# VectorE clips the decays ahead of five of its eight memsets and copies both halves of four heads' queries; heads are turned at the pace of the scores

## The chip, the cores and the metric

The kernel runs on one core of one Trainium2 chip. The metric is the time of one execution in microseconds (us) on the device. Five engines work in parallel, each through its own queue in order: PE (TensorE, matrix products), ACT (ScalarE), DVE (VectorE), POOL (GpSimd) and SP (SyncE, which here only issues transfers). PEld is the loading of weights into PE.

## The reference

Decay attention over 8 batches of 8 heads, 576 positions and 64 dimensions, followed by a two-layer block with a maximum of three products:

```python
def _attn_ref(q, k, v, f):
    scale = 1.0 / np.sqrt(D)
    scores = scale * np.matmul(q, k.transpose(0, 1, 3, 2))
    log_f = np.log(np.clip(f, 0.0001, 1.0))
    cum = np.cumsum(log_f, axis=-1)
    decay = cum[:, :, :, None] - cum[:, :, None, :]
    scores = np.where(causal, -1000000000.0, scores + decay)
    scores = scores - np.max(scores, axis=-1, keepdims=True)
    attn = np.exp(scores)
    attn = attn / (np.sum(attn, axis=-1, keepdims=True) + 1e-09)
    return np.matmul(attn, v)

def _moe_ref(x, w1, w2, w3, w_out):      # x: 4608 x 512, w1..w3: 512 x 768, w_out: 768 x 512
    h = np.maximum(np.maximum(x @ w1, x @ w2), x @ w3)
    return h @ w_out
```

## The kernel before

The program is written as a list of steps. Each step names its engine, an assumed cost, what it reads and writes, and a priority (smaller goes first). A planner (`Plan.emit`) replays the list against these costs, takes on each engine the ready step of the lowest rank, and writes all steps out in order of their planned starts. The queues then run in exactly that order. So one moved priority or dependency changes the order on every engine around it.

The first eight heads (batch 0) go a way of their own. `load_raw` brings a head's keys and queries as they lie in memory (raw tiles, w_111 for head 0 to w_118 for head 7). `turn_head` turns them on PE (L473) into four banks of the accumulator: for even heads queries in mp_130 and keys in mp_131, for odd heads queries in mp_132 and keys in t. Four copies take the two halves of each (e = 0, 1) to the head's tile: before, DVE takes the first half of the queries (L481), ACT the other three (L483). The heads' tiles are qs_65 (head 0), qs_66, ks_67, ks_68 (heads 1 to 3), xh (4, 5) and xl (6, 7). The lower half of each key tile is cleared by a DVE memset (L409), and one of its rows takes the summed decays: for heads 0 and 1 by ACT (L433), for the others by a small transfer (L440) from u_91, which DVE writes at L436.

The decays (pf_80) come from `decay`: two loads, a clip on DVE (L424), a logarithm on ACT (L426), a running sum ("scan") on DVE (L429). ACT loads its tables for logarithm and exponential ahead of need (L421, L428).

Scores of a head are made in two units: unit 2 has queries 0 to 255, unit 1 the rest, in batch 0 in two parts, b (banks s_126, s_127) and then a (bank s_125). Each is: products and mask on PE (L647, L663), maximum over banks on DVE (L702 to L707), maximum over partitions on POOL (L717), a correcting product on PE (L647, from gm_84, gm_85, ph_71 or pl_72), exponentials on ACT (L735), and values on PE (L772), copied out by ACT (L784, and the row of sums L786).

Meanwhile the weights of the two-layer block arrive (L511, tiles w_95 to w_118 in order) and are split into a rounded part and a remainder: ACT L515, DVE L517 and L519, ACT L522, DVE L523. The block's products (L964, L993) are mixed with the attention from then on. The keys and queries of the second batch come as hl, are transposed by DVE (L536) and split (ACT L540, DVE L542). V is loaded by L368, for each pair of heads once the first head's key tile is complete.

Twenty warm-up products (L453, on the identity, into bank s_125) carry priority 90: the planner puts one wherever it believes that PE would be idle. All twenty stand ahead of the first scores in that bank, those of head 0's part a.

Of the kernel before, what the change touches and what calls it, by code (L numbers as in the profile page):

```python
# [48 lines left out]
class Plan:  # L49
# [18 lines left out]
    def add(self, eng, cost, fn, r=(), w=(), prio=0.0, xfer=0.0, rows=128, short=0.0, light=False):  # L68
        i = len(self.steps)
        r, w = ([p for k in keys for p in self.parts.get(k, [k])] for keys in (r, w))  # L70
        deps = set()
        for k in r:
            if k in self.wrote:
                deps.add(self.wrote[k])
        for k in w:
            if k in self.wrote:
                deps.add(self.wrote[k])
            deps.update(self.read.pop(k, ()))
        for k in w:
            self.wrote[k] = i  # L80
        for k in r:
            if k not in w:
                self.read.setdefault(k, set()).add(i)
        deps.discard(i)
        self.steps.append((eng, cost, fn, deps, prio, xfer, rows, short, light))
# [86 lines left out]
def act_cost(cols):  # L172
    return 0.833 * cols + 60


def dve_cost(cols):
    return 1.04 * cols + 68
# [3 lines left out]
def kernel(  # L181
# [15 lines left out]
    nc = tc.nc  # L197
    B, H, S, D = q.shape
    DM, DFF = w1.shape
    P = 128  # L200
# [40 lines left out]
    add = plan.add  # L241
# [9 lines left out]
    KF, QF = [x[:, 0:S] for x in KQ], [x[:, S:] for x in KQ]  # L251
# [115 lines left out]
    def dma(dst, src, r=(), w=(), prio=0.0, bytes_=300000):  # L367
        add("SP", 475 if bytes_ > 200000 else 640, lambda: nc.sync.dma_start(out=dst, in_=src), r, w, prio, bytes_ / 360)  # L368
# [10 lines left out]
    def first_constants(i):  # L379
        nc.gpsimd.memset(QF[i][64:P, :], 1.0)  # L380

    def head_constants(i, prio):

        for key, ns, go in (
# [4 lines left out]
        ):  # L389
            add("POOL", ns, go, w=[key], prio=prio)  # L390

    def value_constants():
        for vn in VN:
            nc.gpsimd.memset(vn[64:P, :, 4, :], 0.0)
            nc.gpsimd.memset(vn[:, :, :, D:D + 1], 1.0)
# [10 lines left out]
    add("POOL", 100, lambda: nc.gpsimd.memset(LESS[0:1].bitcast(F32), -1.0), w=["less"], prio=-9)  # L406
    for i in range(H):
        add("POOL", 525, lambda i=i: first_constants(i), w=[f"qf{i}/2"], prio=-9 + i)
        add("DVE", 605, lambda i=i: nc.vector.memset(KF[i][64:P, :], 0.0), w=[f"kf{i}/2"], prio=-5.5 + 0.1 * i)  # L409
    add("POOL", 1650, value_constants, w=[f"vn{i}" for i in range(4)], prio=-8)  # L410


    def decay():

        fx, lx = PF[1][0:BH + 1, 0:S], PF[1][0:BH + 1, S:2 * S]
        ft = fx[0:BH]
        cs = CS
        fs = f.rearrange("b h s -> (b h) s")

        add("DVE", 60, lambda: nc.vector.memset(TM[0][0:1, 0:1], 1.0), [], ["tm0"], DP)  # L420
        add("ACT", 1400, lambda: nc.scalar.activation(TM[0][0:1, 0:1], TM[0][0:1, 0:1], AF.Ln), ["tm0"], ["tm0"], DP)  # L421
        dma(ft, fs, w=["pf1/0"], prio=DP)
        dma(fx[BH:BH + 1], fs[1:2], w=["pf1/1"], prio=DP, bytes_=2304)
        add("DVE", 440, lambda: nc.vector.tensor_scalar(fx, fx, 1e-4, 1.0, op0=ALU.max, op1=ALU.min),  # L424
            ["pf1"], ["pf1"], DP)
        add("ACT", 600, lambda: nc.scalar.activation(lx, fx, AF.Ln), ["pf1"], ["pf1", "ln"], DP)  # L426

        add("ACT", 1400, lambda: nc.scalar.activation(TM[0][0:1, 0:1], TM[0][0:1, 0:1], AF.Exp), ["ln", "tm0"], ["tm0"], DP)  # L428
        add("DVE", 1275, lambda: nc.vector.tensor_tensor_scan(  # L429
            fx, lx, lx, 0.0, op0=ALU.add, op1=ALU.bypass),  # L430
            ["pf1"], ["pf1"], DP)
        for n in range(2):
            add("ACT", act_cost(S), lambda n=n: nc.scalar.activation(  # L433
                KF[n][D:D + 1, :], fx[BH * n:BH * n + 1, :], AF.Copy, scale=-1.0 / scale), ["pf1"], [f"kf{n}/2"], DP)
        c8 = UT[KT - 1][0:H, :]
        add("DVE", 540, lambda: nc.vector.tensor_scalar(c8, ft[0:H, :], -1.0 / scale, None, op0=ALU.mult),  # L436
            ["pf1"], [f"u{KT - 1}"], DP)
        for n, e, dst in [(n, n + 1, KF[n][64:65, :]) for n in (2, 3)] + [
                (4 + 2 * i, 6 + 2 * i, x[64:65, :, 0:S]) for i, x in enumerate(PAIRS)]:
            add("SP", 560, lambda n=n, e=e, dst=dst: nc.sync.dma_start(out=dst, in_=c8[n:e, :]),  # L440
                [f"u{KT - 1}"], [f"kf{x}/2" for x in range(n, e)], ROWS + n, 2304 / 360)
        add("DVE", 369, lambda: nc.vector.tensor_scalar(cs[:, 0, :], ft, -1.0, None, op0=ALU.mult),
            ["pf1"], ["cs"], DP)
        add("DVE", 669, lambda: nc.vector.scalar_tensor_tensor(
            cs[:, 1, :], ft, -1.0, cs[:, 0, :].bitcast(F32), op0=ALU.mult, op1=ALU.subtract),
            ["pf1", "cs"], ["cs"], DP)
        dma(cdram.bitcast(F32), cs.bitcast(F32), ["cs"], ["cdram"], DP + 3)

    def warm_up():

        z = ident.rearrange("p (o x) -> p o x", o=1).broadcast_to((P, 4, P))
        for _ in range(20):
            add("PE", 217, lambda: nc.tensor.matmul(SP1[0].rearrange("p (o x) -> p o x", o=4), ident, z, start=True, stop=True),  # L453
                ["const"], ["sp1/0"], 90)
        add("DVE", 165, lambda: nc.vector.tensor_copy(IDF, ident), ["const"], ["idf"], -6)
# [8 lines left out]
    def turn_head(n, prio):  # L464


        for c, buf, kc in ((0, QF, "qf"), (1, KF, "kf")):
            ps, kp = ((MPS[0], "mp0"), (MPS[1], "mp1"), (MPS[2], "mp2"), (TPS, "t0"))[2 * (n % 2) + c]

            def go(ps=ps, c=c):  # L470
                for x in range(3):
                    for e in range(2):
                        nc.tensor.matmul(  # L473
                            ps[D * e:D * e + D, 0:288].rearrange("d (p x) -> d x p", x=3)[:, x],
                            RAWQK[n][:, c, e, D * x:D * x + D], IDF[0:96, 0:96], start=x == 0, stop=True, skip_group_check=True)

            add("PE", 700, go, [f"raw{n}/{c}", "idf"], [kp], prio, rows=96)
            for e in range(2):
                dst, src = buf[n][0:D, 288 * e:288 * e + 288], ps[D * e:D * e + D, 0:288]
                if c == 0 and e == 0:  # L480
                    add("DVE", dve_cost(288), lambda dst=dst, src=src: nc.vector.tensor_copy(dst, src), [kp], [f"{kc}{n}/0"], prio)  # L481
                else:
                    add("ACT", act_cost(288) + 115 * e, lambda dst=dst, src=src: nc.scalar.activation(  # L483
                        dst, src, AF.Copy), [kp], [f"{kc}{n}/{e}"], prio)
# [64 lines left out]
    def load_v(pi, prio):  # L549
        b, pr = pi // NP, pi % NP  # L550
        src = v[b, 2 * pr:2 * pr + 2]
        i = pi if b < NB32 else vbuf(pi)
        vn, kv = VN[i], f"vn{i}"

        after = [f"kf{2 * pi}"] if b < NB32 else ["qs0/0"]
        for j in range(2):
            dma(vn[:, j, 0:4, 0:D], src[j, 0:512, :].rearrange("(c p) d -> p c d", p=P),
                after, [kv + f"/{j}"], prio, 262144)
        dma(vn[0:64, :, 4, 0:D], src[:, 512:S, :].rearrange("h p d -> p h d"), after, [kv + "/2"], prio)
# [471 lines left out]
    LEAD, MLAG, WP, WR = 2.1, -0.1, 0.7, 0.65  # L1031
    DP = -10.9
    DPW = 9.0
    ROWS = -4.0
    warm_up()
    decay()
    QP = -0.3
    UO = 1
# [7 lines left out]
    for n in range(H):  # L1046
        load_raw(n, n - 8.9)
    for n in range(H):
        turn_head(n, n - 5.6)
        if n % 2 == 0:  # L1050
            load_v(n // 2, n - LEAD - VP)
    for unit, up in ((2, 0.0), (1, 0.1)):
# [94 lines left out]
```

## Time and profile before

| what | value |
|---|---|
| median of 3 runs | 903.28 us |
| lowest, highest | 903.13, 905.31 us |
| span of the profiled execution | 900.3 us |
| PE busy | 889.3 us (99%) |
| DVE, ACT, POOL busy | 624.8, 389.0, 425.8 us |
| transfers | 110.99 MB, mean 123 GB/s |

The profile is of one execution on one core; its span runs from the first to the last instruction. For the profiled execution no other time than its span is given; the median of the runs is 3.0 us above it. Rows of a timeline show the start in us, the duration in us, the engine, the line, the operation, what is written and read, how many instructions of a kind were merged, and in brackets how long the engine had been idle before and what ended that. Rows of waits show the total in us, how often, and the longest.

### The profile page before, as it was taken

To read this page: it belongs to the slowest core of one execution; us is meant where nothing else is said; L and a number is where in the kernel's file an instruction comes from. 1 tells how busy PE (TensorE), PEld (TensorE's weight loads), DVE (VectorE), ACT (ScalarE), POOL (GpSimd) and SP (SyncE) were. 2 spreads that over 40 slices of the span, in tenths; PEclk is the share of its full clock that TensorE was granted. 3 is DMA by queue.
4 is the path that set the end of the run, shared out by engine and by line. 5 is a ranking of instruction groups with operands and counts; after the bars stand their busy time and mean duration, and the time that the engine had idled before them with its cause. 6 is when DMAs were issued, how large, how long until landed. Compare 5 with 4: busy or idle time off the path is not lost.

```text
span 900.3 us, 18339 instructions
## 1 busy us (share of the span) xinstructions
PE 889.3 (99%) x6646; PEld 804.0 (89%) x6646; DVE 624.8 (69%) x1419; ACT 389.0 (43%) x904; POOL 425.8 (47%) x380
## 2 busy tenths in 40 slices
PE   8999999999999999999999999999999999999998
PEld 6899989888889899989989998998989898998998
DVE  6999954667759786877849787786958677672211
ACT  6898543433334443443334443344433533442111
POOL 4543232245555756556464755555565564650000
PEclk9999999999999999999999999999999999999999
DMA  7994265554464454446445445536434555401000
GB/s 197 316 270 133 56 159 131 147 135 127 99 189 96 124 136 118 126 100 169 96 124 149 117 133 138 140 93 181 95 102 123 126 149 118 105 15 37 1 36 24
DMA packets 98155, 110.99 MB, mean 123 GB/s; under 512 B 52637, under 2 KB 65693, under 8 KB 98066
## 3 DMA queue, kind: packets, MB, share of 16 engines
q1 hardware_dynamic: 98066, 109.83, 46.7%
q8 instruction: 53, 0.87, 0.4%
q14 instruction: 36, 0.29, 0.1%
HBM read 50.22 MB, written 9.87 MB: 67 GB/s over the span
## 4 chain that ended last, share of the span: by engine, by line
PE 92%; ACT 3%; DMA 1%; DVE 1%; SPq 1%; issue 1%; DVEq 0%; ACTq 0%
PE mp L964 51%; PE mp L993 17%; PE s L647 12%; PE t L803 9%; PE t L772 2%; PE t L822 1%; DMA w<-in_moe_w_dram 1%; ACT w L515 1%; ACT pf L735 1%; SPq L368 1%; DMA r_r<-rdram 0%; ACT ph L786 0%; ACT w_r L522 0%; PE s L663 0%; ACT u L784 0%
## 5 line engine op out<-in xcount | busy, mean ns | idle before, releaser
L964 PE MATMUL mp<-xh_r,w_r 128*128 128x320 f32 (+1 forms) x2160 | 463.5, 298 | 1.7 <-DVE tm L973 1.4
L964 PEld LDWEIGHTS mp<-xh_r,w_r 128*128 128x128 f32 x2160 | 356.1, 188 | 11.2 <-issue 5.6
L964 PE MATMUL mp<-xl_r,w_r 128*128 128x320 f32 (+1 forms) x1080 | 319.6, 296 | 0.4 <-DVE xl_r L940 0.4
L759 POOL PARTITION_ALL_REDUCE z<-va_s x96 | 194.9, 2030 | 158.4 <-DVE va_s L751 57.4
L717 POOL PARTITION_ALL_REDUCE gm<-mx x131 | 156.6, 1196 | 206.8 <-DVE mx L707 88.9
L964 PEld LDWEIGHTS mp<-xl_r,w_r 128*128 128x128 f32 x1080 | 203.3, 188 | 1.1 <-DVE xl_r L940 0.6
L973 DVE TENSOR_TENSOR tm<-mp,tm 128x256 f32<-128x256 f32 (+1 forms) x192 | 86.5, 451 | 84.6 <-PE mp L964 79.4
L647 PE MATMUL s<-qs_r,ks_r 128*128 128x320 f32 (+4 forms) x784 | 133.1, 284 | 0.2 <-issue 0.2
L647 PEld LDWEIGHTS s<-qs_r,ks_r 128*128 128x128 f32 (+1 forms) x784 | 116.9, 181 | 18.2 <-issue 13.4
L993 PE MATMUL mp<-w_r,hmh_r 128*128 128x512 f32 (+1 forms) x396 | 122.7, 392 | 0.0
L707 DVE TENSOR_TENSOR mx<-mx,s 128x320 f32<-128x320 f32 (+3 forms) x248 | 92.3, 372 | 19.5 <-PE s L647 6.9
L993 PEld LDWEIGHTS mp<-w_r,hmh_r 128*128 128x128 f32 x396 | 70.2, 188 | 13.2 <-issue 1.4
L976 ACT ACTIVATE hmh_r<-tm 128x256 fp32r<-128x256 f32 x96 | 39.9, 416 | 97.0 <-DVE tm L973 96.1
L993 PE MATMUL mp<-w_r,hml_r 128*128 128x512 f32 (+1 forms) x198 | 76.8, 388 | 0.0
L971 ACT ACTIVATE tm<-mp 128x256 f32<-128x256 f32 (+1 forms) x96 | 39.6, 413 | 82.3 <-PE mp L964 78.0
L536 DVE STREAM_TRANSPOSE hl<-hl 128x576 f32<-128x576 f32 x56 | 68.7, 1242 | 8.1 <-DMA hl<-in_k_dram 5.3
L735 ACT ACTIVATE pf<-s 128x512 f32<-128x512 f32 (+4 forms) x107 | 49.4, 506 | 30.5 <-PE s L647 26.4
L978 DVE TENSOR_TENSOR hml_r<-tm,hmh_r 128x256 fp32r<-128x256 f32 x96 | 48.2, 502 | 18.5 <-ACT hmh_r L976 17.9
L720 POOL CAST qs_r<-gm 1x256 fp32r<-1x256 f32 (+1 forms) x112 | 56.0, 500 | 7.2
L676 DVE TENSOR_TENSOR s<-s,mask 128x256 f32<-128x256 f32 x96 | 40.8, 425 | 25.8 <-PE s L647 25.5
L714 ACT ACTIVATE mx<-s 128x320 f32<-128x320 f32 (+1 forms) x64 | 26.7, 417 | 58.4 <-DVE s L681 45.1
L735 ACT ACTIVATE ph_f<-s 128x384 f32<-128x384 f32 x80 | 36.1, 505 | 36.1 <-PE s L647 36.1
(209 smaller groups left out, 1227.9 us busy)
## 6 DMA issues: line engine op xcount, KB each, us to landing
qs_r<-hl SPq DMA_DIRECT2D x168, 144.0 KB
ks_r<-hl SPq DMA_DIRECT2D x168, 144.0 KB
w<-in_moe_w_dram SPq DMA_DIRECT2D x18, 512.0 KB
out_dram<-o_r SPq DMA_DIRECT2D x35, 256.0 KB
hl<-in_q_dram SPq DMA_DIRECT2D x14, 576.0 KB
hl<-in_k_dram SPq DMA_DIRECT2D x14, 576.0 KB
r_r<-rdram SPq DMA_DIRECT2D x56, 144.0 KB
vn<-in_v_dram SPq DMA_DIRECT2D x30, 128.0 KB
```

The lines of the kernel that those rows point to most:

```text
L536: add("DVE", 1085, lambda e=e, tt=tt, xs=xs: nc.vector.transpose(tt[:, e], xs[:, e]), [key + "0"], [key + "1"], prio)
L647: nc.tensor.matmul(bank[bk][0:l.shape[-1], col:col + w], l, rhs(qa, w), start=start and bk not in begun, stop=stop, skip_group_check=True)
L707: nc.vector.tensor_tensor(mt[:, a:a + w], mt[:, a:a + w], bank[bk][:, col:col + w], op=ALU.max)
L717: add("POOL", 450 + 2.6 * nq, lambda: nc.gpsimd.partition_all_reduce(gm, mt, P, bass.bass_isa.ReduceOp.max), [km, km + "a"], [kg], prio - CB)
L720: add("POOL", 130 + 0.9 * nq, lambda: nc.gpsimd.tensor_copy(QS(s)[96:97, 1, q0:q0 + nq], gm[96:97, :]), [kg], [kx], prio - CB)
L735: add("ACT", act_cost(w), lambda bk=bk, w=w, col=col: nc.scalar.activation(px()[:, col:col + w], bank[bk][:, 0:w], AF.Exp, scale=sc), [kb[ ...
L759: add("POOL", 520 + 5.1 * nq, lambda: nc.gpsimd.partition_all_reduce(Z[:, q0:q0 + nq], blocks_sum()[:, q0:q0 + nq], P, bass.bass_isa.Reduc ...
L803: nc.tensor.matmul(t[D * j:D * j + D, qa:qa + w], vn[:, j, c, 0:D], prs[j][0]()[:, col:col + w], start=x == 0, stop=True, skip_group_check ...
L964: nc.tensor.matmul(m, unit_w(i, fb)[:, w, kt, :], xx, start=kt == 0 and x == 0, stop=kt == KT - 1 and x == 2,)
L973: add("DVE", dve_cost(cn), lambda m=m: nc.vector.tensor_tensor(t, m, t, op=ALU.max), [km, kt_], [kt_], prio)
L978: add("DVE", dve_cost(w), lambda hh=hh, hl=hl, a=a, d=d, w=w: nc.vector.tensor_tensor(hl()[:, fb, d:d + w], t[:, a:a + w], hh()[:, fb, d:d ...
L993: nc.tensor.matmul(mp[:, 0:cn], l[:, fb, cs], unit_o(fb)[:, r, ds], start=fb == 0 and x == 0, stop=fb == FT - 1 and x == 2,)
```

## The change

Three edits. The memsets of the key tiles of heads 3 to 7 now depend on the decays: that of head 3 comes behind the clip, those of heads 4 to 7 behind the scan. For heads 0 to 3, DVE copies both halves of the queries, and ACT only the keys. Heads 2 to 7 are turned with a priority that follows that of their scores (0.5 a head) and no longer one of 1.0 a head.

```diff
+    def key_rows(i, after):
+        add("DVE", 605, lambda i=i: nc.vector.memset(KF[i][64:P, :], 0.0), after, [f"kf{i}/2"], -5.5 + 0.1 * i)
+
...
     for i in range(H):
         add("POOL", 525, lambda i=i: first_constants(i), w=[f"qf{i}/2"], prio=-9 + i)
-        add("DVE", 605, lambda i=i: nc.vector.memset(KF[i][64:P, :], 0.0), w=[f"kf{i}/2"], prio=-5.5 + 0.1 * i)
+        if i < 3:
+            key_rows(i, [])
...
         add("DVE", 440, lambda: nc.vector.tensor_scalar(fx, fx, 1e-4, 1.0, op0=ALU.max, op1=ALU.min),
-            ["pf1"], ["pf1"], DP)
+            ["pf1"], ["pf1", "clip"], DP)
         add("ACT", 600, lambda: nc.scalar.activation(lx, fx, AF.Ln), ["pf1"], ["pf1", "ln"], DP)
+        key_rows(3, ["clip"])
...
         add("DVE", 1275, lambda: nc.vector.tensor_tensor_scan(
             fx, lx, lx, 0.0, op0=ALU.add, op1=ALU.bypass),
-            ["pf1"], ["pf1"], DP)
+            ["pf1"], ["pf1", "scan"], DP)
+        for i in range(4, H):
+            key_rows(i, ["scan"])
...
-                if c == 0 and e == 0:
-                    add("DVE", dve_cost(288), lambda dst=dst, src=src: nc.vector.tensor_copy(dst, src), [kp], [f"{kc}{n}/0"], prio)
+                if c == 0 and (e == 0 or n < 4):
+                    add("DVE", dve_cost(288) + 100 * e, lambda dst=dst, src=src: nc.vector.tensor_copy(dst, src),
+                        [kp], [f"{kc}{n}/{e}"], prio)
...
+    TURN = 1.3
...
     for n in range(H):
-        turn_head(n, n - 5.6)
+        turn_head(n, n - 5.6 if n < 2 else 0.5 * n - LEAD - TURN)
```

The changed order starts on every engine with the turns and ends about a fifth into PE's rows; behind that it is the same. In the rows below each line begins with the line of the kernel; lines after the new function stand some numbers higher in the changed kernel (L409 is L393, L424 L428, L429 L434, L481 L488, L483 L491, L473 L480, L647 L655, L735 L743, L515 L523, L784 L792, L453 L460).

The first place is DVE's queue from its third memset on. Before:

```order
L409 MEMSET ks_67 64x576
L455 CAST hdl<-ident 128x128
L409 MEMSET ks_68 64x576
L409 MEMSET xh 64x576 x2
L424 TENSOR_SCALAR pf_80<-pf_80 65x576
L409 MEMSET xl 64x576 x2
L429 SCALAR_TENSOR_TENSOR pf_80<-pf_80 65x576
L436 TENSOR_SCALAR u_91<-pf_80 8x576
L481 COPY qs_65<-mp_130 64x288
L481 COPY qs_66<-mp_132 64x288
L481 COPY ks_67<-mp_130 64x288
```

The same stretch of DVE's queue in the changed kernel:

```order
L393 MEMSET ks_67 64x576
L462 CAST hdl<-ident 128x128
L428 TENSOR_SCALAR pf_80<-pf_80 65x576
L393 MEMSET ks_68 64x576
L434 SCALAR_TENSOR_TENSOR pf_80<-pf_80 65x576
L488 COPY qs_65<-mp_130 64x288
L443 TENSOR_SCALAR u_91<-pf_80 8x576
L488 COPY qs_65<-mp_130 64x288
L393 MEMSET xh 64x576 x2
L488 COPY qs_66<-mp_132 64x288 x2
L393 MEMSET xl 64x576 x2
L488 COPY ks_67<-mp_130 64x288 x2
```

Clip and scan passed five memsets; the two pairs of heads 4 to 7 now stand between the copies of heads 0, 1 and 2.

The second place is ACT's queue from head 7's copies (xl from t and mp_132) to the first weights, with the values of head 0 (u_88) between. Before:

```order
L735 ACTIVATE pf_81<-s_128 128x384
L483 ACTIVATE xl<-mp_131 64x288
L515 ACTIVATE w_95<-w_95 128x512
L483 ACTIVATE xl<-t 64x288 x2
L483 ACTIVATE xl<-mp_132 64x288
L515 ACTIVATE w_96<-w_96 128x512
L522 ACTIVATE w_r<-o 128x512
L784 ACTIVATE u_88<-t 64x160
```

The same stretch of ACT's queue in the changed kernel:

```order
L491 ACTIVATE xl<-t 64x288 x2
L491 ACTIVATE xl<-mp_132 64x288
L548 ACTIVATE hl<-hl 128x1152
L792 ACTIVATE u_88<-t 64x160
L794 ACTIVATE ph_79<-t 1x160
L743 ACTIVATE pf_80<-s_126 128x480
L792 ACTIVATE u_88<-mp_132 64x256
L794 ACTIVATE ph_79<-mp_132 1x256
L743 ACTIVATE pf_80<-s_127 128x224
L743 ACTIVATE hmh<-mp_130 128x384
L743 ACTIVATE hml<-mp_131 128x384
L523 ACTIVATE w_95<-w_95 128x512
```

The first weight moved from ahead of head 7's copies to behind three heads' exponentials. On SP's queue its load moved with it: before, it was issued right behind the loads of hl (queries, then keys); now the loads of V for heads 2 and 3 (hdh) and 4 and 5 (vl), the store of the decays (cdram) and the key part of hl stand between the query part of hl and w_95, and the query part stands ahead of the V loads of heads 2 and 3.

The third place is PE's queue around turn 2 (w_113) and the first scores of head 0 (from qs_65). Before:

```order
L453 MATMUL s_125<-ident 128x512
L473 MATMUL mp_130<-hdl,w_113 64x96 x6
L473 MATMUL mp_131<-hdl,w_113 64x96 x6
L473 MATMUL t<-hdl,w_114 64x96 x6
L473 MATMUL mp_132<-hdl,w_114 64x96 x6
L647 MATMUL s_126<-qs_65 128x160 x3
```

The same stretch of PE's queue in the changed kernel, from turn 1 (w_112) on:

```order
L480 MATMUL mp_132<-hdl,w_112 64x96 x6
L480 MATMUL mp_130<-hdl,w_113 64x96 x6
L480 MATMUL mp_131<-hdl,w_113 64x96 x6
L655 MATMUL s_126<-qs_65 128x160 x3
L655 MATMUL s_127<-qs_65 128x160
L655 MATMUL s_127<-qs_65 128x64
```

Turn 3 (w_114) moved behind the first scores, and the five warm-up products that stood between turns 1 and 2 are gone from there. Of the twenty, seven still stand at the start; before, five stood between turns 1 and 2, three between head 7's turn and the first values, and five behind the first values; now two stand in turn 5, one ahead of the first values, and ten behind them, the last two right ahead of head 0's part a.

## The prediction

> **What bounds the kernel now.** I read the first part of the page, a table of stages, the waits of PE and the chain that ended last, in that order, and then the timelines of the first 35 us.
>
> ```profile
> PE 889.3 (99%) x6646; PEld 804.0 (89%) x6646; DVE 624.8 (69%) x1419; ACT 389.0 (43%) x904; POOL 425.8 (47%) x380
> ...
> 0.00:5.00 5.00, 3.47 (x11) 1.26 (x13) 3.51 (x8) 1.49 (x2) 3.54 (x20) 1.00 0.46 127
> 5.00:10.00 5.00, 3.72 (x53) 2.75 (x49) 4.55 (x7) 4.09 (x7) 4.94 (x8) 1.00 0.92 249
> 45.00:50.00 5.00, 5.00 (x45) 4.97 (x45) 4.80 (x13) 4.88 (x13) 2.93 (x4) 1.00 1.10 335
> 50.00:60.00 10.00, 10.00 (x83) 9.38 (x81) 9.77 (x21) 9.77 (x23) 5.75 (x7) 1.00 0.95 232
> 80.00:90.00 10.00, 10.00 (x88) 10.00 (x88) 9.18 (x20) 6.72 (x17) 2.58 (x3) 1.00 0.12 31
> ```
>
> PE is busy 99% of the span, so a gain can only come from the 11 us in which it is not, or from warm-up products that delay real ones. The stages (PE, PEld, DVE, ACT, POOL, clock, DMA share, GB/s) show where: the first 10 us. From 45 to 60 us PE, DVE and ACT are all full at once; from 80 us ACT has slack and PE alone carries the time.
>
> ```profile
> PE mp L473 <- ACT qs L483: 1.6, 1, 1.6
> PE t L772 <- ACT pf L735: 1.1, 2, 0.5
> ...
> PE s L647 <- ACT pf L735: 0.3, 1, 0.3
> ...
> 1.39 1.80 DMA pf<-in_f_dram
> 5.00 0.70 DVE pf L424
> 7.06 1.36 DVE pf L429
> 18.04 6.81 DMA w<-in_moe_w_dram
> 24.87 0.68 ACT w L515
> 63.20 0.61 ACT pf L735
> 63.84 1.15 PE t L772 x8
> ```
>
> The chain starts with the decays: they land at 3.19, are clipped only at 5.00 and scanned at 7.06, pass SP's queue, and reach PE by way of the first weight, which lands 6.81 us after its issue at 18.04. Until 63.84 the chain runs mostly through ACT, then through PE to the end. What the change is worth is thus decided before about 64 us; behind that PE's work is the same and nearly in the same order.
>
> **PE's lost time before.** From the end of the second head's turn (6.87 + 0.66 = 7.53):
>
> ```profile
> 1.53 3.17 PE L453 MATMUL s<-ident 128*128 128x512 bf16 x7 [1.53 <-POOL ident masks.py:199]
> 6.87 0.66 PE L473 MATMUL mp<-hdl,w 96*64 96x96 f32 x12
> 7.46 1.25 PE L453 MATMUL s<-ident 128*128 128x512 bf16 x5
> 10.31 1.21 PE L473 MATMUL mp<-hdl,w 96*64 96x96 f32 x24 [1.59 <-ACT qs L483]
> 12.73 1.52 PE L647 MATMUL s<-qs 128*128 128x160 f32 x10
> 17.23 0.74 PE L647 MATMUL s<-gm,pl 128*128 128x160 f32 x5
> 24.84 0.75 PE L647 MATMUL s<-gm,pl 128*128 128x160 f32 x5
> 26.46 1.42 PE L772 MATMUL t<-pf,vn 128*65 128x64 f32 x10 [0.65 <-ACT xl L483]
> 28.55 0.82 PE L453 MATMUL s<-ident 128*128 128x512 bf16 x3
> 29.39 0.60 PE L453 MATMUL s<-ident 128*128 128x512 bf16 x2
> 29.83 1.12 PE L647 MATMUL s<-qs 128*128 128x160 f32 x8
> ```
>
> Between 7.53 and 10.31 only five warm-up products run: 2.78 us. Between 25.59 (24.84 + 0.75) and 26.46: 0.87. Five more warm-up products at 28.55 and 29.39, at 1.25 / 5 = 0.25 each: 1.25. The waits for L735: 1.4. In all 6.3 us, 0.7% of the span. No reordering can win more than that.
>
> **The change, step by step.**
>
> ```profile
> 3.83 1.15 DVE L409 MEMSET xh<- 64x576 f32 x2
> 9.07 0.79 DVE L481 COPY qs<-mp 64x288 f32<-64x288 f32 x2
> 12.30 0.45 DVE L481 COPY ks<-mp 64x288 f32<-64x288 f32 x1 [2.43 <-ACT ks L483]
> 14.67 0.64 DVE L704 TENSOR_REDUCE mx<-s 128x160 f32<-128x480 f32 x1
> 5.74 0.68 ACT L426 ACTIVATE pf<-pf 65x576 f32<-65x576 f32 x1 [3.51 <-DVE pf L424]
> 8.45 1.37 ACT L433 ACTIVATE qs<-pf 1x576 f32<-1x576 f32 x2
> 9.85 0.84 ACT L483 ACTIVATE qs<-mp 64x288 f32<-64x288 f32 x2
> 24.87 0.68 ACT L515 ACTIVATE w<-w 128x512 f32<-128x512 f32 x1 [4.03 <-DMA w<-in_moe_w_dram]
> 29.03 0.30 ACT L784 ACTIVATE u<-t 64x160 f32<-64x160 f32 x1
> 31.88 1.19 ACT L540 ACTIVATE hl<-hl 128x1152 fp32r<-128x1152 f32 x1
> 16.09 2.39 POOL L717 PARTITION_ALL_REDUCE gm<-mx  x2 [5.94 <-DVE mx L707]
> 17.13 0.39 SPq L368 DMA_DIRECT2D hl<-in_q_dram  x1
> 19.78 2.74 SPq L368 DMA_DIRECT2D vl<-in_v_dram  x3
> ```
>
> *Clip first.* Ahead of the clip now stand three memsets and the cast; it can start when the decays are in, 3.2 instead of 5.0. The logarithm follows 0.74 behind it as now (5.74 - 5.00), so at 3.96 to 4.64; one memset (1.15 / 2) fits beside it; the scan runs 4.7 to 6.1, not 7.06 to 8.4. ACT's two decay rows (L433) follow at 6.2 to 7.5, 2.3 us earlier, then the two copies of head 0's keys (0.84) to 8.4. DVE takes both halves of head 0's queries, with L436 between them, by 7.7. Head 0 is ready at 8.4, not at 10.7 (9.85 + 0.84).
>
> *The memsets behind.* Their sum is unchanged. The pairs for heads 4 to 7 (1.15 each) now stand on DVE ahead of the copies of heads 1 and 2, whose free banks PE needs for turns 3 and 4. The cover is DVE's 2.43 of waiting at 12.30; without it the first maximum (L704) would be later by as much. By DVE's queue: xh pair to 8.8, head 1 to 9.6, xl pair to 10.8, head 2 to 11.7, so L704 at 11.7 instead of 14.67.
>
> *Four copies from ACT to DVE.* ACT loses 4 x 0.42 = 1.7 us (0.84 / 2 each), DVE gains 4 x 0.45 = 1.8. Before 22 us both wait more than that. In the full stage DVE is no fuller for it, since all four stand ahead of it.
>
> *Turns at the scores' pace.* PE now goes from turn 2 (7.7 to 9.1) straight to head 0's scores, at about 9.1 instead of 12.73; head 3's turn, 1.2, follows later. POOL's reduction, which had waited 5.94, starts at 13.0 instead of 16.09, and the correction pass (17.23 now) runs at about 15.6, where the same turns are done: 1.6 us ahead. POOL's other moved steps lie in its waits.
>
> *ACT's wait on the first weight.* ACT now copies head 7 ahead of any weight. The 4.03 us for w_95 no longer stand between head 7's turn and the first values, so these start right behind the second correction pass and a product: about 23.9 instead of 26.46. Lead: 2.5 us.
>
> *SP's queue.* The batch's first query load passes key load, weights and V: 14 instead of 17.13. Three V loads of 2.74, the decays' store and the key load now pass the first weight: I put its issue at 20.4 instead of 18.04. ACT needs it behind L540 and the group that ran from 29.03 to 31.88 and a half us on: 24.2 + 1.2 + 3.0 = 28.4; with the same 6.81 it lands at 27.2. Hidden, by 1.2 us.
>
> *Given back.* Thirteen warm-up products instead of eight stand after the start, ten of them, not five, behind the first values, and head 0's part a (bank s_125) may not begin before the last. If PE is full, that costs 5 x 0.25 = 1.25 us; if PE would wait anyway, nothing: I take 0.75. That part starts about 5 us later than 29.83, and its exponentials then stand on ACT among weight steps of 0.6 to 0.7. No row shows those waits. At best the present 1.4 us go too; at worst each of the eight heads waits once for one such step, 8 x 0.63 = 5.0, so 3.6 more. I take 0.5 more, near the present rows, because ACT's stretch also begins some 2.5 us of work ahead.
>
> Sum: -2.5 + 0.75 + 0.5 = -1.25 us. The profiled span is 900.3; the median of the runs, 903.28, is 3.0 longer, which I carry unchanged: 902.0. The ends: -2.5 - 1.4 = -3.9 (899.4) and -2.5 + 1.25 + 3.6 = +2.35 (905.6).
>
> **A rule against it.** Seven warm-up products took 3.17 us from 1.53, 0.45 each, but 0.25 each at 7.46: PE began at about half rate, although the granted clock reads 1.00. If taking the five away let PE fall back, work of some 3.4 us would double its time at most once, +1.7. Now PE waited 1.59 there and its next turns ran at full rate (0.66 for twelve), and the new pause is about 1 us. The Trainium skill, "TensorE: Matmul & The Clock Gate", Part 1, says that the array's clock halves after an idle window of about 3.4 us, in windows that run freely. By that rule the pause expected here is too short; the trace agrees, as far as 1.59 us goes.
>
> **The rivals.**
> 1. *The lead comes through whole.* The extra products fall into waits, and ACT, begun earlier and with 1.7 less to do, no longer holds PE up. For it: PE waits for ACT alone after 24 us. Against: ACT is at 98% from 45 to 60. 2.5 plus 0.8 of the 1.4: 900.0.
> 2. *Slower: ACT waits for weights again.* Place: L515 on w_95, in ACT's queue ahead of the copies (L784) that free the bank of the next values. For it: 4.03 now, and an issue 2.4 us later. Against: its need is 3.5 us later as well. It decides from an issue later than 21.6 (28.4 - 6.81). A wait as now of 4.0 gives 902.0 + 4.0 = 906.0.
> 3. *The start doesn't move.* The DMA engines are at 0.92 from 5 to 10 us; if head 2's data land only near 10, turn 2 stays where it is: 903.3.
> 4. *The clock falls back:* 902.0 + 1.7 = 903.7.
>
> **How the numbers follow.** The forecast has 0.47, rival 1 0.30, rival 2 0.13, rival 3 0.07, rival 4 0.03. Time 902.0, on its own 900.6 to 903.9. A measurement tells about 0.3%, 2.7 us, from no change: faster means below 900.6. Most of rival 1 lies there, and a tail of the forecast: 0.29. Slower is rival 2 and the forecast's worst end: 0.13. Same: 0.58. The range goes down to the fast end, 899.4, and up to 904.9, which leaves most of rival 2 outside.
>
> **What would show it.** Clip near 3.2, scan near 4.7, head 0's scores near 9.1, first values near 23.9 with no ACT wait for w ahead of them. From 30 to 70 us, PE's waits for L735 and L784 tell the forecast (about 2 us) from rival 1 (under 1). An ACT wait for w above 1 us is rival 2; turn 2 at 10 is rival 3; rows at twice their length near 8 to 12 us are rival 4. The forecast is wrong if values start later than 25, or if the full stage loses more than 2.5 us.

## The result, and the profile after

The changed kernel is slower: 912.43 us, median of six runs (909.68 to 914.34), against 903.20 for the kernel before (six runs beside it). The ratio is 1.0092, 95% interval 1.0068 to 1.0115. The forecast was 902.0, range 899.4 to 904.9. The traced execution took 911.97 us; its span is 909.9 us against 900.3, so 9.6 us are to be explained.

The page's first part and four stages of the changed kernel, then the same stages of the kernel before where the prediction has not shown them (PE, PEld, DVE, ACT, POOL busy, granted clock, DMA share, GB/s):

```profile
PE 893.4 (98%) x6646; PEld 807.1 (89%) x6646; DVE 631.5 (69%) x1423; ACT 386.8 (43%) x900; POOL 421.6 (46%) x380
```

```profile
5.00:10.00 5.00, 2.85 (x58) 2.37 (x56) 4.76 (x5) 4.16 (x8) 4.91 (x8) 1.00 0.92 254
40.00:45.00 5.00, 2.47 (x20) 2.10 (x19) 4.97 (x13) 4.14 (x10) 2.53 (x2) 1.00 1.09 348
...
210.00:220.00 10.00, 9.45 (x52) 8.28 (x52) 6.05 (x15) 4.09 (x11) 5.14 (x4) 0.66 0.37 85
```

```profile
40.00:45.00 5.00, 5.00 (x45) 4.85 (x43) 4.97 (x10) 4.77 (x13) 3.24 (x3) 1.00 1.11 278
...
210.00:220.00 10.00, 10.00 (x74) 9.54 (x73) 7.10 (x20) 3.80 (x11) 6.69 (x5) 1.00 0.54 161
```

Three places differ: PE loses 0.9 us more from 5 to 10, has half of 40 to 45 idle (DVE is equally full in both), and from 210 to 220 is busy but at a granted clock of 0.66.

The whole run can be followed by one group that comes back for each pair of heads: the 20 products of the values (L803 before, L811 after, 2.21 us in both). The starts below are from the chain of each kernel; the last column is the span.

| kernel | 1st group | 4th group | 6th group | span |
|---|---|---|---|---|
| before | 114.26 | 178.56 | 236.62 | 900.3 |
| changed | 119.39 (+5.1) | 183.90 (+5.3) | 246.48 (+9.9) | 909.9 (+9.6) |

So nothing is lost before the first values (26.60 against 26.46; the lead of 2.5 is simply missing), 5 us behind them, and 4.5 more between the 4th and the 6th group. The 4th and the 6th group are fair marks: PE has run the same number of products by then in both kernels (1550 and 1970). By the 1st group the changed kernel has run six more of the block's, about 1 us at the 0.12 to 0.23 that one of them takes in a row, so some 4 of the 5 us are lost by then. The waits of PE in the changed kernel (total, times, longest) name the places:

```profile
PE mp L972 <- ACT xh_r L946: 2.3, 1, 2.3
PE mp L480 <- DVE qs L488: 2.1, 1, 2.1
PE mp L866 <- DVE u L877: 1.6, 2, 1.1
...
PE mp L866 <- ACT rx L859: 1.5, 1, 1.5
```

**Place 1, the start.** Timeline rows of DVE, then of PE, in the changed kernel:

```profile
3.50 0.46 DVE L428 TENSOR_SCALAR pf<-pf 65x576 f32<-65x576 f32 x1 [0.46 <-DMA pf<-in_f_dram]
...
4.70 1.35 DVE L434 TENSOR_TENSOR_SCAN pf<-pf 65x576 f32<-65x576 f32 x1
6.09 0.46 DVE L488 COPY qs<-mp 64x288 f32<-64x288 f32 x1
6.47 2.56 DVE L443 TENSOR_SCALAR u<-pf 8x576 f32<-8x576 f32 x1
9.07 0.45 DVE L488 COPY qs<-mp 64x288 f32<-64x288 f32 x1
...
14.00 0.64 DVE L712 TENSOR_REDUCE mx<-s 128x160 f32<-128x480 f32 x1
```

```profile
9.57 1.21 PE L480 MATMUL mp<-hdl,w 96*64 96x96 f32 x24 [2.13 <-DVE qs L488]
10.71 1.52 PE L655 MATMUL s<-qs 128*128 128x160 f32 x10
...
18.29 0.74 PE L655 MATMUL s<-gm,pl 128*128 128x160 f32 x5
...
26.60 1.37 PE L780 MATMUL t<-pf,vn 128*65 128x64 f32 x10
...
37.59 1.12 PE L655 MATMUL s<-qs 128*128 128x160 f32 x8
...
42.00 0.71 PE L866 MATMUL mp<-hdl,rx 128*128 128x128 f32 x4 [1.45 <-ACT rx L859]
42.47 0.60 PE L655 MATMUL s<-gm,pl 128*128 128x160 f32 x4
44.15 0.68 PE L866 MATMUL mp<-hdl,rx 128*128 128x128 f32 x4 [1.08 <-DVE u L877]
```

Clip and scan came forward as foreseen (3.50, 4.70). Then L443, 0.69 us before as L436, takes 2.56 on eight partitions, and the second half of head 0's queries waits behind it; PE gets turn 2 at 9.57. The row before, with the POOL row beside it:

```profile
8.45 0.69 DVE L436 TENSOR_SCALAR u<-pf 8x576 f32<-8x576 f32 x1
```

```profile
7.74 1.09 POOL L380 MEMSET xl<- 64x576 f32 x2
```

**Place 2, 37 to 46 us.** Head 0's part a (scores of 1.12 us at 29.83 before) starts at 37.59, behind the last warm-up product. The spreading of the sums (L866) then waits 1.45 and 1.08 us for steps of ACT (L859) and DVE (L877) that come late through DVE's queue, where weight steps stand ahead (L531 at 40.70, L525 and L527 from 42.24 to 43.67).

**Place 3, the end of the second batch.** The chain there:

```profile
201.02 0.83 PE s L655 x7
201.85 0.51 SPq L575
...
202.42 0.64 SPq L575
...
203.11 0.58 SPq L575
...
203.80 0.54 SPq L881
...
204.38 4.39 DMA r_r<-rdram
...
208.86 0.77 DVE u L941
...
209.65 0.69 ACT xh_r L946
...
210.37 0.77 DVE xl_r L948
```

The loads of r_r (L881, the attention's sums, taken by way of memory) stand in SP's queue behind head loads (L575) that wait for PE's scores. Before, they were issued at 196.53:

```profile
196.53 0.54 SPq L873
...
197.12 4.23 DMA r_r<-rdram
```

After the wait the products are slow, 0.47 to 0.64 instead of 0.31, as a finer table of stages shows: half the clock from 210 to almost 217.

```profile
208.00:210.00 2.00, 0.11 (x2) 0.00 (x0) 0.76 (x1) 0.35 (x1) 1.87 (x2) 0.99 0.92 237
210.00:212.00 2.00, 1.45 (x4) 1.05 (x5) 0.96 (x2) 1.02 (x3) 0.12 (x1) 0.50 0.26 57
212.00:214.00 2.00, 2.00 (x10) 2.00 (x10) 0.99 (x3) 0.44 (x1) 1.67 (x1) 0.50 0.00 0
214.00:216.00 2.00, 2.00 (x10) 2.00 (x9) 0.86 (x3) 1.14 (x3) 1.38 (x2) 0.50 0.00 0
216.00:218.00 2.00, 2.00 (x13) 2.00 (x12) 1.57 (x4) 0.79 (x4) 0.08 (x1) 0.81 0.64 149
```

The changed order of instructions ends at about 215 us; the prediction had looked at its consequences only up to 64.

### The profile page after: what moved, and what is told of

Its sections match the earlier page's. It is cut to its first block, busy times and chain, and to the rows that moved or that the text cites. A ratio compares the mean times of both kernels' runs of the same rounds, so it can differ in the third digit from the quotient of the medians.

```text
span 909.9 us, 18363 instructions
## 1 busy us (share of the span) xinstructions
PE 893.4 (98%) x6646; PEld 807.1 (89%) x6646; DVE 631.5 (69%) x1423; ACT 386.8 (43%) x900; POOL 421.6 (46%) x380
## 4 chain that ended last, share of the span: by engine, by line
PE 94%; DVE 3%; ACT 1%; DMA 0%; issue 0%; SPq 0%; POOL 0%; DVEq 0%; POOLq 0%; ACTq 0%
PE mp L972 51%; PE mp L1001 17%; PE s L655 13%; PE t L811 9%; PE t L780 2%; PE t L830 1%; DMA r_r<-rdram 0%; PE s L460 0%; PE mp L780 0%; PE mp L480 0%; PE s L671 0%; PE mp L655 0%; DVE mx L712 0%; DVE u L443 0%; DVE w_r L531 0%
## 5 line engine op out<-in xcount | busy, mean ns | idle before, releaser
L655 PEld LDWEIGHTS s<-qs_r,ks_r 128*128 128x128 f32 (+1 forms) x784 | 117.1, 182 | 19.0 <-issue 14.2
L655 PE MATMUL s<-qs_r,ks_r 128*128 128x320 f32 (+4 forms) x784 | 133.3, 286 | 0.0
L743 ACT ACTIVATE pf<-s 128x512 f32<-128x512 f32 (+4 forms) x107 | 48.8, 505 | 26.4 <-PE s L655 25.7
L728 POOL CAST qs_r<-gm 1x256 fp32r<-1x256 f32 (+1 forms) x112 | 53.8, 482 | 7.0
L743 ACT ACTIVATE ph_f<-s 128x384 f32<-128x384 f32 x80 | 36.1, 505 | 42.3 <-PE s L655 42.2
```

The source lines that it names most:

```text
L655: nc.tensor.matmul(bank[bk][0:l.shape[-1], col:col + w], l, rhs(qa, w), start=start and bk not in begun, stop=stop, skip_group_check=True)
L728: add("POOL", 130 + 0.9 * nq, lambda: nc.gpsimd.tensor_copy(QS(s)[96:97, 1, q0:q0 + nq], gm[96:97, :]), [kg], [kx], prio - CB)
L743: add("ACT", act_cost(w), lambda bk=bk, w=w, col=col: nc.scalar.activation(px()[:, col:col + w], bank[bk][:, 0:w], AF.Exp, scale=sc), [kb[ ...
```

## Experiments

### Which stretch of the order loses

Theory T: the order behind the first values loses. Theory S: the start loses. Theory C: the clock alone. The planner is replaced by an order written out: that of one kernel up to a point, that of the other behind it.

```diff
-        for i in sorted(range(n), key=lambda j: (begin[j], j)):
-            self.steps[i][2]()
+        for x in ORDER:
+            self.steps[at[x]][2]()
```

**Start changed, the rest as before** (o_abb).

> The instructions up to the first values stand in the order of the changed kernel, all behind them in the order of the kernel before (the five warm-up products that have no place left are dropped). Theory T (the loss sits in the order behind the first values: 5 us up to about 110 us, 2 to 4 more where the second batch ends at about 200 us): first values at 26.6 as in the changed kernel, the 20-product group of values at 159.3 to 160.3 (before 159.34, changed 164.38), span 900 to 902, ratio to before 0.998 to 1.003. Theory S (the start itself loses, by the DVE product L443 that took 2.56 us instead of 0.69 and what comes late through it): values group at 162 to 164.4, span 903 to 906 and more. Theory C (the granted clock alone): span 900, whatever the order.

**Only the stretch from the first values to 125 us changed** (o_bab).

> Start as in the kernel before, then the order of the changed kernel up to a planned time of 115 us (some 125 us on the chip), then the order of the kernel before. Theory T: head 0's part a is held behind the warm-up products, PE waits at 38 to 45 us, the values group comes at 163 to 164.5, span 904 to 906, ratio 1.004 to 1.006. Theory S: no loss, values group at 159.3 to 160, span 900 to 901.5.

**Only what lies behind 125 us changed** (o_bba).

> The order of the kernel before up to a planned time of 111 us, then that of the changed kernel. Theory T: values group at 159.3 to 160, then PE waits about 2 us for L946 near 205 us and the granted clock may fall there, span 902 to 906, ratio 1.002 to 1.006. Theory S: span 900 to 901.5 with no such wait. Theory C: the wait alone without a fall of the clock would show span 902.

| kernel | ratio | 95% | 4th group | 6th group | span |
|---|---|---|---|---|---|
| o_abb | 0.9988 | 0.9977 to 0.9999 | 179.64 (+1.1) | 236.98 (+0.4) | 901.2 |
| o_bab | 1.0052 | 1.0040 to 1.0065 | 184.33 (+5.8) | 242.38 (+5.8) | 906.0 |
| o_bba | 1.0033 | 1.0020 to 1.0046 | 181.56 (+3.0) | 242.67 (+6.1) | 906.5 |

The three add up to 1.0073, against 1.0092 (1.0068 to 1.0115) for the whole change. T holds for the place of the loss: the start gains at most 0.2% (and o_abb leaves out five warm-up products, 1.25 us or 0.14%, which may be all of it), the middle costs about 0.5%, the second batch's end about 0.3%, there with a wait of 1.8 for L946. That part a's late start is the cause within the middle these three don't show, since that stretch changed as a whole.

The spans of o_bab and o_bba hold a loss that is not theirs. Both start in the order of the kernel before, and in both traces PE waited longer for head 7's copies, behind the first weight, than the 0.65 of the first trace (1.42 and 1.59), and the granted clock read 0.50 from 28 to 30. So o_bba is 1.9 late at its 1st group already (116.19), where its order is still that of the kernel before; from the 4th group to the 6th it loses 3.1. For o_bab the ratio of the runs, 0.5%, is the better measure.

S falls, since the changed start alone loses nothing. C, the clock alone, falls too, but the clock has a part: the one execution of the changed kernel with a mean granted clock of 1.000 has a span of 907.8, sixteen such executions of the kernel before lie between 899.1 and 904.2, the middle one near 901. So some 7 of the 9 us remain without any fall of the clock, and about 2 come through it.

### The warm-up products that hold part a

**The changed kernel with ten of them.**

```diff
-        for _ in range(20):
+        for _ in range(10):
```

> The changed kernel with ten warm-up products instead of twenty; the planner makes its order anew. Theory T: head 0's part a no longer waits for them and its scores stand before 30 us (changed 37.59, before 29.83), the PE waits at 40 to 45 us go, span 898 to 904, ratio 0.995 to 1.004. Theory S: the start is unchanged and so is the loss, span 906 to 910.

Measured 0.9983 (0.9973 to 0.9993), span 900.2; part a's scores at 28.92, no PE wait above 1.0 from 28 to 60 us, no wait for L946. The new plan changes much else, so the mirror was run as well: **the kernel before with 24.**

> The kernel before with 24 warm-up products instead of 20; the planner makes its order anew, and in it head 0's part a falls behind the group of products it followed, as in the changed kernel. Theory T (part a, held behind the last warm-up product, is what costs 5 us in the stretch from 25 to 125 us): part a's scores at 36 to 38 instead of 29.83, PE waits of 2 us and more for L859 and L877 at 40 to 46 us, the first of the 20-product groups behind 100 us 4 to 6 us later than before (114.26), span 904 to 909, ratio 1.004 to 1.010. Rival (four more products are four more products): 1 us, span 901 to 902, ratio 1.000 to 1.002.

Measured 1.0120 (1.0093 to 1.0147), span 913.5, above the range that I gave. PE's rows of that kernel:

```profile
30.33 1.25 PE L453 MATMUL s<-ident 128*128 128x512 bf16 x5
...
37.36 0.38 PE L453 MATMUL s<-ident 128*128 128x512 bf16 x1
37.57 1.12 PE L647 MATMUL s<-qs 128*128 128x160 f32 x8
```

Five run in a row at 30.33, one is left, and part a waits for it until 37.57. The rival (1 us for four products of 0.25) is out as a price of the new count, but the 11 us are not the price of part a alone, since the planner made a new order. Between 205 and 215 us PE waits 3.9 for L938, and behind that the clock is at half for some 7 us: more than half of the loss lies there. The first group comes at 122.97 (+8.7), but 24 more of the block's products and the four warm-up products stand ahead of it, some 6 us of work (0.12 to 0.25 each in a row). The waits that I had named at 40 to 46 came in another form, 0.6 for the exponentials of L735; the stretch was less idle than in the changed kernel (PE busy 8.31 of 10 from 40 to 50, there 7.30, before 10.00). No run moves part a alone, so what its late start costs by itself stays open.

### L443 beside POOL's memsets

**The order of the changed kernel with L443 moved** (DVE's queue):

```diff
 L488 COPY qs_65<-mp_130 64x288
-L443 TENSOR_SCALAR u_91<-pf_80 8x576
 L488 COPY qs_65<-mp_130 64x288
 L393 MEMSET xh 64x576 x2
 L488 COPY qs_66<-mp_132 64x288 x2
+L443 TENSOR_SCALAR u_91<-pf_80 8x576
```

> The order of the changed kernel with one instruction moved: DVE's L443 (u_91) stands behind the copies of head 1's queries, at about 9.2 us, when POOL's row of memsets (to 8.7) is over. If L443 is slow because it runs beside those memsets: it takes 0.3 to 0.5 there instead of 2.56, the second half of head 0's queries is copied at 6.5, turn 2 starts at 7.4 to 8.3 instead of 9.57, head 0's scores at 8.7 to 9.5 instead of 10.71, the correction pass at 16 to 17.3 instead of 18.29. If it is slow by itself, it takes 2.5 again. Theory T says that the loss behind the first values stays: span 906 to 909.5, ratio to before 1.004 to 1.009. Theory S says that the loss goes: span 900 to 902.

Its DVE rows, POOL's rows beside them, and the same instruction in the kernel with the first edit alone (below):

```profile
6.07 0.92 DVE L488 COPY qs<-mp 64x288 f32<-64x288 f32 x2
...
9.18 0.95 DVE L443 TENSOR_SCALAR u<-pf 8x576 f32<-8x576 f32 x1
```

```profile
7.61 1.09 POOL L380 MEMSET xl<- 64x576 f32 x2
8.76 1.06 POOL L401 MEMSET ph<- 97x1152 f32 x1
```

```profile
6.08 2.95 DVE L443 TENSOR_SCALAR u<-pf 8x576 f32<-8x576 f32 x1
```

L443's end is fixed by POOL, not by its start: begun at 6.08, 6.47 or 6.62 it ends at 9.02 or 9.03, 0.3 after the L380 memsets (8.71 to 8.73 in those traces); begun at 9.18 it ends at 10.13, 0.3 after L401 (9.82). Its own work is thus at most about 0.3. It did not take 0.3 to 0.5 in its new place, since L401 was in the way, but nobody waits for it there. The first half of turn 2 was done at 8.02, head 0's scores came at 9.09, the correction pass at 16.63, first values at 24.93, 1.7 us earlier than in the changed kernel and 1.5 earlier than before. At the 1st group 0.65 of the 1.7 is left (118.74); in this trace the clock read 0.50 from 44 to 46, so that eight value products took 2.08 instead of 1.15 and eight scores 1.79 instead of 1.12. The ratio is 1.0068 (1.0048 to 1.0088). T again: the losses behind the start stay (waits of 1.4 and 1.1 for L859 and L877, 2.1 for L946).

The Trainium skill, "SBUF — State Buffer", section "Who interferes with whom", says that a single-source tensor_scalar on VectorE from SBUF to SBUF can take the port pair that it shares with GpSimd, and that the one that comes second blocks until the other's instruction is finished. The trace agrees in kind; here the wait lasted over a row of memsets (6.47 to 8.73 in the changed kernel), not one.

### The rows of sums behind the head loads

**The order of the changed kernel with SP's queue changed near 200 us:**

```diff
+L881 DMA rdram<-sc 2x32x8
+L881 DMA rdram<-sc 2x32x10
 L1009 DMA out_dram<-o_r 128x512
-L881 DMA rdram<-sc 2x32x8
-L881 DMA rdram<-sc 2x32x10
+L881 DMA r_r<-rdram 64x576 x2
 L575 DMA qs_r<-hl 32x2x576
 L575 DMA ks_r<-hl 32x2x576
 L575 DMA qs_r<-hl 32x2x576
-L881 DMA r_r<-rdram 64x576 x2
```

> The order of the changed kernel with one output store and two loads moved in SP's queue near 200 us: the sums' rows (L881 to rdram) stand ahead of the store of o_r (L1009), and the loads of r_r (L881) ahead of three head loads (L575). Theory T: r_r is issued at 201 to 202 instead of 203.8, PE's wait for L946 falls from 2.3 to under 0.8, and without that wait the granted clock stays at 1.00 between 200 and 220 (changed 0.83): span 904 to 907, ratio 1.003 to 1.006. If the clock falls there for another reason, the wait goes but the span is 907 to 909. If the head loads moved back are needed at once, PE waits for them instead: no change, 909.5 to 910.5.

Measured 1.0050 (1.0031 to 1.0069), against 1.0092. The wait for L946 is gone from the table (what is left of it is 0.6 for L948), the clock stays up:

```profile
210.00:215.00 5.00, 4.43 (x29) 3.96 (x29) 3.20 (x8) 3.02 (x9) 4.57 (x5) 1.00 0.12 26
```

From the 4th to the 6th group it takes 244.05 - 185.41 = 58.6 us; the changed kernel 62.6, the kernel before 58.1. So 3.9 of the 4.5 lost at place 3 hang on the place of a few rows of a DMA queue, the fall of the clock behind the wait included. The span itself was above my range (908.4), since this execution had lost 1.5 us more by its 1st group, up to which the clock fell twice (between 10 and 16 us and between 44 and 50).

**The kernel before with its loads of r_r two head loads later:**

> The kernel before with one thing worsened: in SP's queue the loads of r_r at 196.5 us stand behind the next two head loads instead of ahead of them (some 2.6 us later). PE then waits about 3 us for L946 near 204 us instead of 0.7. If such a wait makes PE's rate fall, the products behind it (L972, 0.31 each) take 0.47 and more for some us, the granted clock between 200 and 220 falls below 1.00, and the span is 905 to 907, ratio 1.004 to 1.008. If the fall in the changed kernel has another cause, the span is 902 to 903.5, ratio 1.002 to 1.004.

Measured 1.0011 (0.9996 to 1.0027), against my 1.004 to 1.008. Its trace, though, lost 3.75 us by the 6th group (240.37), with a wait of 2.6 and a clock of 0.74 and 0.50 from 206 to 210. A second trace was taken, and two more of the kernel before and one of the changed kernel, to see whether the fall is a matter of chance:

> A second trace of the kernel with the later loads of r_r. If the fall of the rate follows the wait each time: wait 2 to 3 us, L972 at 0.47 for some us behind it, span 903 to 905. If the fall is a matter of chance: the wait without it, span 901 to 902.

> The order of the kernel before, written out: nothing is changed, and a second trace of it is wanted. If PE's rate falls near 205 us in this kernel too, in some executions (waits 0.7 there), a trace with a span of 902 and more shows L972 at 0.47 and a granted clock below 1.00 between 200 and 220; if the rate never falls here, the span is 900 to 901 or the loss lies elsewhere.

> As the other look at the kernel before: a third trace of it.

> A second trace of the changed kernel. Traces of three kernels with the same start showed head 0's scores at 2.5 to 2.8 us instead of 1.52; if that is the usual case, they take 2.5 here too, and the 20-product groups come 1 us later than in the first trace (119.39); at the second batch's end again a wait of about 2 us for L946.

The second trace of the worsened kernel shows a wait of 1.5 and no fall: 236.98 at the 6th group, span 900.6. The kernel before never fell near 205 in three traces, but it fell elsewhere in two of them: in one at 12.5 to 16 us, where it cost nothing (1st group at 114.19, span 900.2), in one at 30 to 34, with the 1st group at 117.82 (+3.6) and a span of 903.4. There the clock is the smaller part: PE had waited 3.20 us for head 7's copies instead of 0.65, because the first weight came 2.65 later on ACT (27.52 for 24.87). So the wait that the change removes varies from execution to execution. The row of the wait, and two stages of that trace:

```profile
29.09 1.53 PE L780 MATMUL t<-pf,vn 128*65 128x64 f32 x10 [3.20 <-ACT xl L491]
```

```profile
30.00:33.00 3.00, 3.00 (x14) 2.12 (x12) 3.00 (x6) 2.52 (x7) 0.00 (x0) 0.55 0.95 237
33.00:36.00 3.00, 3.00 (x22) 2.77 (x21) 1.74 (x2) 2.93 (x6) 0.62 (x1) 0.89 1.05 309
```

In the second trace of the changed kernel (span 912.5) the clock fell three times: head 0's scores took 2.82 us instead of 1.52, behind the waits at 40 to 45 it read 0.50 from 46 to 48, and behind a wait of 2.8 near 212 it was at half again. Two stages of the first fall:

```profile
10.00:12.00 2.00, 2.00 (x25) 1.88 (x22) 1.71 (x5) 0.81 (x2) 0.03 (x1) 0.67 1.14 239
12.00:14.00 2.00, 2.00 (x15) 1.88 (x16) 1.88 (x5) 0.00 (x0) 0.00 (x0) 0.50 0.67 140
```

Of five traces with the changed start unmended (changed twice, o_abb, warm10, the SP rows) four show scores of 2.53 to 2.82. Of nine traces with the five warm-up products at 7.5, two do (2.50 and 2.82, of the kernel with the later loads and of the kernel before); the two with L443 moved do not. So the pause of 1.4 to 2.2 us at 8 to 9.6 usually costs 1.0 to 1.3 us more in the changed start. A wait of 1.8 to 4.4 near 205 to 215 was followed by a fall in each of nine traces. How long a wait must be is not settled, and length alone does not decide: near 205 us 1.5 passed and 1.8 did not, behind a wait of 1.4 ahead of the first values o_bab's rows took 2.61 instead of 1.42, and at the start pauses of 1.5 fell while 1.8 (the later loads) and 2.1 (changed, first trace) passed.

### Each edit alone

Two of the three edits were taken out of the changed kernel each time, and the planner made its order anew. Memsets behind clip and scan alone:

> The kernel before with the first edit alone: the memsets of heads 3 to 7 behind the clip and the scan. L443 then stands ahead of head 0's copy and should again last until POOL's memsets are over (8.7 to 9.1), whenever it starts. Theory T: no lead at the start, part a behind the last of the warm-up products at 36 to 38 us, span 904 to 909, ratio 1.004 to 1.009. Theory S (the edits are good or bad by the start alone): 899 to 901.

DVE's copies alone:

> The kernel before with the second edit alone: DVE copies both halves of the queries of heads 0 to 3. By the planned order part a stands late here too. Theory T: scores of part a at 36 to 38, span 904 to 909, ratio 1.004 to 1.010. Theory S: 900 to 902.

The turns' pace alone:

> The kernel before with the third edit alone: heads 2 to 7 turned at the pace of the scores. In the planned order part a stands early, as before. Theory T: part a at 29.5 to 31, no PE wait above 1 us between 35 and 60 us, span 899 to 903, ratio 0.997 to 1.003. If the order at the second batch's end is what decides: 902 to 906 with a wait for L946 near 205.

| edit alone | ratio | 95% | part a's scores | PE's wait at 205 to 215 us |
|---|---|---|---|---|
| memsets behind | 1.0111 | 1.0090 to 1.0132 | 38.30 | 2.0 |
| DVE's copies | 1.0114 | 1.0091 to 1.0138 | 38.01 | 4.4 |
| turns' pace | 1.0072 | 1.0049 to 1.0095 | 29.50 | 2.7 |

(The wait is that for the rounded part of x, L946 or L942.) The first two behave as T says in part a's time and in their sign, and lost more than I wrote; their waits near 210 belong to the second batch's end. The third refutes T as a complete account: part a is early, yet PE waits 1.6 for head 1's exponentials at 32.30, 3.1 us are idle from 60 to 80, and the second batch's end loses as elsewhere. Every order that the planner made anew lost there, but that with ten warm-up products: the order before had its loads of r_r at a good place, and I know of nothing in the planner that keeps them there.

### A version that beats both

**Ten warm-up products, and L443 behind the copies of head 1:**

> Ten warm-up products, and L443 behind the copies of head 1's queries: both remedies together, the order otherwise that of the kernel with ten. If the start's lead comes through now: first values 1 to 2 us earlier than 27.07, span 898 to 899.5, ratio to before 0.995 to 0.997. If ACT's stretch from 40 to 70 us takes it back: span 900, ratio 0.998 as without the move.

Measured 901.01 us, ratio 0.9964 (0.9953 to 0.9975), span 899.4; first values at 25.03, 2.0 earlier than without the move (where the trace also had a fall of the clock at 10 to 14); 6th group at 233.19 (-3.4, of which about 1 us are nine products that stand behind it here). The kernel is faster than the one before by 0.36%, in the ratio what rival 1 of the prediction gave for the change, but it also runs ten warm-up products fewer.

## Why the prediction was wrong, step by step

- *Clip first*: right to 0.3 us (3.50 and 4.70 for 3.2 and 4.7).
- *DVE's row of copies by 7.7*: **the step that failed first.** I priced L436 at 0.69 from its row before. That row ended at 9.14, 0.3 behind POOL's memsets (8.83), like the later ones: by that, more than half of it was a wait. Begun earlier it only waited longer, 2.56. Head 0 ready at 9.5 for 8.4, turn 2 at 9.57 for 7.7, L712 at 14.00 for 11.7, correction pass 18.29 for 15.6, first values 26.60 for 23.9. Lead: 0 for 2.5 (26.60 against 26.46 before). With L443 out of the way 1.5 of it came (24.93).
- *ACT's wait for the first weight*: right. It is gone, the weights' first step at 30.88 follows without one (issue at 21.63 for my 20.4). Rival 2 did not happen.
- *Rival 3* (raw data late) did not happen: with L443 moved, half of turn 2 was done at 8.02.
- *Given back*: **the term that was mis-sized most.** I took 0.75 for warm-up products and 0.5 for waits, 1.25 in all; 5.3 was lost by the 4th group, and about 0.5% in time. I had foreseen part a 5 us later than 29.83, it was 7.8; and I had let only ACT's exponentials wait. What waited was the spreading of the sums (L866), behind a full DVE, 2.5 us at 40 to 45; five more products at 0.25 are 1.25. The rest, some 1.5, is not traced to a row.
- *"What the change is worth is decided before about 64 us"*: **wrong.** The order differs up to 215 us, and a few rows on SP cost 4 us there in the traces, and some 2 in executions whose mean clock stayed at 1.000 (spans of 907.8 and, with the rows moved, 905.8 to 906.2). No term stood for it, and no rival.
- *Rival 4* (the clock, 0.03, 1.7 us): five of the six executions have a mean granted clock below 1.000; in the traces it fell at the start for 1.0 to 1.3 us, at 45 and at 210. I judged the pause at 1 us; it was 2.1 and 1.5. Doubling 3.4 us of work would cost 3.4 and not 1.7; what the traces show is 3.4 us at half rate, which is 1.7 of lost work, so the price stands. The Trainium skill, "TensorE: Matmul & The Clock Gate", Part 1, speaks of an idle window of about 3.4 us. Here waits of 1.4 to 2.8 us were enough in some traces, and half rate lasted about 3.4 or 6.8 us (0.50 from 210 to 216 and 0.81 in the next 2), one or two such windows.

The sign of the sum was thus lost for three reasons: no lead, a middle about 4 us worse than priced, and a place 140 us behind the edits that was not priced at all.

## What to carry to other kernels

Where a planner writes the order, a local edit has to be read in the order up to the last differing row, on the DMA queue too; splicing two orders at a chosen point shows which stretch pays, by the ratio of many runs more than by one trace. A filler of lowest priority that writes the bank of a step of high priority holds that step back to the last filler (part a at 37.59 for 29.83): give it a bank that nobody needs, or few enough of it. Before pricing an instruction from its row, see what else ends when it ends.

## What the hardware showed that I had not expected

A DVE instruction on 8 x 576 elements took 0.69, 0.95, 1.42, 2.56 and 2.95 us in five places, and ended each time 0.3 us behind a POOL memset. DVE's memsets, its copies from the accumulator (0.46) and its scan (1.35) ran beside the same POOL memsets at their usual length. The clip, the same operation on 65 x 576, took 0.70 before and 0.46 in the changed kernel; the pair of POOL memsets that it overlapped before took 1.40, and 1.09 in the changed kernel, where the clip was over by then.

Waits of PE of about 2 us, shorter than I took to be harmless, let its clock fall to 0.50 for 3.4 us or twice that, not in each execution. One such stretch at half rate is 1.7 us of lost work at most, and two of them are what separates a mean clock of 1.000 from one of 0.996: with L443 moved the spans were 905.5 at 1.000 and 908.4 at 0.996.
